# First constant on ScalarE's queue, transposes of w_out one item later, and a second copy buffer for the norm of w_in

## The chip, the cores and the metric

The kernel runs on one core of one Trainium2 chip. The metric is the device time of one execution in microseconds (us). Before the change it took 1651.17 us, the median of 3 runs (1646.57 to 1651.53). One execution was recorded by the hardware profiler; it took 1647.89 us, and its span, from the first instruction to the last, is 1646.1 us.

Engine names: PE is TensorE's matmul, PEld its weight load, ACT is ScalarE, DVE is VectorE, POOL is GpSimd, SP is SyncE, which here only issues DMAs (SPq in the trace). ACT issues DMAs too (ACTq).

## The reference, cut to what matters

```python
# batch 8, seq 3072, dim 256; float32 in and out
X  = rfft(x, axis=1)                        # along the sequence
Yr = shrink(Xr @ w_r - Xi @ w_i + b_r)      # shrink: sign(v) * max(|v| - 0.01, 0)
Yi = shrink(Xr @ w_i + Xi @ w_r + b_i)
a  = irfft(Yr + 1j * Yi, axis=1)            # 24576 tokens x 256
y  = (s * relu(a @ w_in) ** 2 + b) @ w_out  # w_in 256x2048, w_out 2048x256
e  = argmax(y @ w_gate)                     # 8 experts; at most 768 tokens of each are kept
out = gate * (relu(y @ w1[e]) @ w2[e])      # for the tokens kept, zero for the rest
```

The inputs w_in and w_out come as 64-bit floats, so the kernel turns their words into 32-bit floats itself, piece by piece.

## The kernel before, in words

All instructions are issued in the order in which the Python code emits them; every engine works through its own queue in that order, and waits stop the whole queue. A tile with a tag and a number of buffers waits until the oldest tile with that tag has been used up.

**The head (lines 1686 to 1701).** `f1_load(0, t)` loads the 16 slices of the first batch on SP's queue (192 KB each). `load_consts` then loads the constant `f1` (96x96 floats, 36 KB; `f<-c_f` in the trace) and `f1t`, and `load_moe` three small inputs, all on SP's queue. `f1_mm(0, t)` multiplies a slice by `f1` on PE (two passes of 512 columns), ACT or DVE in turn copies the result to a tile `z`, and SP writes it to DRAM (`zd<-z`). After slice 4 a 512 KB load of `d` stands on SP's queue, after slice 7 the two 256 KB loads of `wm`. Then come `warm(18)`, matmuls on zeros, and `group_items(0)`: 12 groups, each of which loads `zp` from what was written to `zd`, transforms, mixes with w_r and w_i, and transforms back. The first load of `zp` needs all 16 slices written.

**The conversion of the weights.** `conv_items(seq, ahead)` makes a list of items; item n issues the load of piece n+ahead, then `conv_low` of piece n+1 (two ACT passes over the raw words, which wait for the load), then for w_in `conv_use` of piece n, or for w_out `conv_tr` of piece n-1 (a DMA of the piece to `wd` on SP, 4 transposes on PE into `pwt`, a copy `wt` on ACT) and `conv_gate` of piece n-2 (16 matmuls with w_gate, a transpose on DVE), and last `conv_word` of piece n+1 (four DVE operations, L543 to L550, and two POOL operations, L551 and L552, which finish the piece `cf`). The 8 pieces of w_in (CONV_A) run beside the groups. The list for the 8 pieces of w_out (CONV_B) has 12 items: the first two are issued at the end of the groups, the other ten stand in slots 0, 0, 1, 2, 3, 3, 4, 5, 6, 6 of the next stage (MOE_CONV_AT), in front of all else in their slot. `load_bias` follows in slot 7.

**The first units of the next stage.** For batch 0 a loop runs over 64 slots; in slot k `s_unit` multiplies a tile of tokens by a part of w_in on PE (`ph`), squares the relu on ACT and DVE (`r`, `qb`), and then the slot's other work follows: conversion items, the norm of w_in, from slot 4 the loads of the next batch, from slot 6 its `f1_mm`.

**The norm of w_in** (`gram_items`) is 32 items spread over slots 0 to 9: 16 times `turn` (4 transposes on PE into `pwg`, a copy `wgt` on ACT, one buffer) and `add` (4 matmuls of `wgt` by itself into `gram`), in the order turn 0, add 0, turn 1, add 1 and so on. After the 8th and the 16th `add`, ACT squares `gram` into a tile `gsq` of its own and DVE sums it.

Of the kernel before, what the change touches and what calls it, by code (L numbers as in the profile page):

```python
# [10 lines left out]
F32 = mybir.dt.float32  # L11
F32R = mybir.dt.float32r
# [8 lines left out]
N1 = 96  # L21
# [3 lines left out]
NF = FF // 128  # L25
# [20 lines left out]
CONV_B = tuple(range(8))  # L46
# [102 lines left out]
class Kern:  # L149
# [11 lines left out]

    def load_consts(self, cp):
        nc, I = self.nc, self.I
        self.f1 = cp.tile([N1, 96], F32, tag="f1", name="f1")
        nc.sync.dma_start(out=self.f1, in_=I["c_f1"])
        self.f1t = self.mo.tile([96, N1], F32, tag="f1t", name="f1t")
        nc.sync.dma_start(out=self.f1t, in_=I["c_f1t"])
        self.d = cp.tile([128, G, 128], F32, tag="d", name="d")
        self.e = cp.tile([128, G, 128], F32, tag="e", name="e")
        self.wm = [cp.tile([128, 2, C], F32, tag=f"wm{k}", name=f"wm{k}") for k in range(4)]  # L170
        self.bias = [cp.tile([128, C], F32, tag=f"bias{k}", name=f"bias{k}") for k in range(2)]
        self.l20 = cp.tile([128, 2, 32], F32, tag="l20", name="l20")
        nc.vector.memset(self.l20, 0.0)
# [309 lines left out]
    def cbuf(self, what, k):  # L483

        if what == "r":
            if k not in CONV_A:
                pool, tag, n = self.wk, "x", 4
            else:
                pool, tag, n = (self.mo, "cr", 1) if CONV_A.index(k) % 3 == 2 else (self.mo, "u", 3)
            return pool.tile([128, 512, 2], I32, tag=tag, name="cr", bufs=n)  # L490
        dt = F32 if what in "fm" else I32
        if k in CONV_A:
            if what == "f":
                return self.stage()[:, :512]
            pool = self.mo
            tag, n = dict(t=("ah", 2), p=("asq", 2), m=("cm", 2))[what]
        else:
            pool = self.wk
            tag, n = dict(t=("z", 4), p=("sl", 2), m=("v", 3), f=("zp", 3))[what]
        return pool.tile([128, 512], dt, tag=tag, name="c" + what, bufs=n)  # L500

    def conv_load(self, k):
# [80 lines left out]
                                 start=(h == 0), stop=(h == 1), skip_group_check=True)  # L583
        nc.vector.transpose(out=self.wog[:, 2 * k:2 * k + 2], in_=pg[:, 0:64].rearrange("p (k f) -> p k f", k=2))

    def conv_items(self, seq, ahead):
        def at(f, n):
            if 0 <= n < len(seq):
                f(seq[n])

        def step(n):
            at(self.conv_load, n + ahead)
            at(self.conv_low, n + 1)
            for f, lag in ((self.conv_use, 0), (self.conv_tr, 1), (self.conv_gate, 2)):
                if 0 <= n - lag < len(seq) and (seq[n - lag] < 8) == (lag > 0):
                    f(seq[n - lag])
            at(self.conv_word, n + 1)
        return [lambda n=n: step(n) for n in range(-ahead, len(seq) + (2 if seq[-1] < 8 else 0))]

    def load_bias(self, pp):  # L600
# [18 lines left out]
    def gram_items(self):  # L619


        nc = self.nc

        def turn(k, f):
            ps = self.psum("pwg")
            for m in range(4):
                ff, c = divmod(m, 2)
                nc.tensor.transpose(ps[:, m * 128:(m + 1) * 128],
                                    (self.win, self.wl)[k].bitcast(F32)[:, c, (f + ff) * 128:(f + ff + 1) * 128], self.ident)
            t = self.wk.tile([128, 2, 2 * 128], F32R, tag="kw", name="wgt", bufs=1)  # L630
            nc.scalar.copy(out=t.rearrange("p a c -> p (a c)"), in_=ps)
            self.wgt = t

        def add(k, f):
            if f == 0:
                self.gram = self.lp.tile([128, 512], F32, tag="lg", name="gram")
            for ff in range(2):
                for c in range(2):
                    nc.tensor.matmul(self.gram[:, c * 256:(c + 1) * 256], self.wgt[:, ff, c * 128:(c + 1) * 128], self.wgt[:, ff],
                                     start=(f + ff == 0 and c == 0), stop=(f + ff == NF - 1), skip_group_check=True)  # L640
            if f == NF - 2:
                sq = self.wk.tile([128, 512], F32, tag="kw2", name="gsq", bufs=1)
                nc.scalar.activation(out=sq, in_=self.gram, func=AF.Square)
                nc.vector.tensor_reduce(out=self.nrm[:, k:k + 1], in_=sq, axis=AX.X, op=ALU.add)
        it = []
        for k in range(2):
            for f in range(0, NF, 2):
                it += [lambda k=k, f=f: turn(k, f), lambda k=k, f=f: add(k, f)]
        return it

    def bound_items(self, pp, diff=False):
# [1003 lines left out]
    def run(self):  # L1655
        tc, nc, B = self.tc, self.nc, self.B
# [4 lines left out]
        with ExitStack() as es, tc.manual_schedule():  # L1661
# [6 lines left out]
            cp = e2.enter_context(tc.tile_pool(name="cp", bufs=1))  # L1668
# [18 lines left out]
            self.wl = pp.tile([128, 2, FF], F32R, tag="wl", name="wl")  # L1687
            self.zero = zero = pp.tile([128, C], F32, tag="zero", name="zero")
            nc.vector.memset(zero, 0.0)
            for t in range(16):  # L1690
                self.f1_load(0, t)
            self.load_consts(cp)
            self.load_moe(pp)
            conv = self.conv_items(CONV_A, 3)
            f1 = self.f1_items(0)
# [14 lines left out]
            for k, f in enumerate(gr):  # L1710
                f()
                if k in extra:
                    extra[k]()
                if k in FFT_CONV_AT:
                    conv.pop(0)()
                if not conv:
                    conv = self.conv_items(CONV_B, 2)
            self.warm(WARM_GROUPS)
            self.i2_load(0, 0)
            self.i2_load(0, 1)  # L1720
# [28 lines left out]
            for b in range(B):  # L1749
# [60 lines left out]
                for k in range(64):  # L1810
                    i, u = divmod(k, 8)
# [3 lines left out]
                    if k in ZERO_AT:  # L1815
                        for zi in range(math.ceil(nz * nzi / nzn), math.ceil(nz * (nzi + 1) / nzn)):
                            nc.sync.dma_start(out=ov[zi].rearrange("p (a c) -> p a c", a=2),
                                              in_=zero.unsqueeze(1).to_broadcast([128, 2, C]))
# [60 lines left out]
```

## Time and profile before

| | before |
|---|---|
| median of the runs | 1651.17 us (1646.57 to 1651.53, 3 runs) |
| the profiled execution | 1647.89 us, span 1646.1 us |
| PE busy | 1471.8 us (89% of the span), 9469 matmuls |
| PE weight loads | 1217.3 us (74%) |
| DVE / ACT / POOL busy | 953.6 (58%) / 814.1 (49%) / 268.1 us (16%) |
| moved by DMA | 230.03 MB, mean 140 GB/s |
| mean granted clock of TensorE | 0.966 |

PE is the busiest engine, and in most of the span its share is near full. A share says nothing of what a stage waits for: that is read from the waits and from the order of time. A granted clock of 1.00 is 2.4 GHz, 0.50 is 1.2 GHz; a matmul takes about twice as long at the lower one, and counts as busy for that long.

### The profile page before, as it was taken

How to read it: one execution, taken by the hardware profiler on the slowest of the kernel's cores; microseconds unless marked ns; L12 is line 12 of the kernel's file. 1: busy time of each engine (PE TensorE's matmuls, PEld its weight loads, DVE VectorE, ACT ScalarE, POOL GpSimd, SP SyncE). 2: the span in 40 equal slices, each digit the busy share in tenths (PEclk: the TensorE clock that was granted, in tenths of full speed). 3: DMA queues.
4: the chain of work that ended last, by engine and by line, in shares of the span. 5: the costliest groups of instructions: out<-in, count | busy, mean ns of one | idle time of the engine just before them, and what ended most of it. 6: DMA issues, size and time to landing. Idle time of an engine off the chain costs nothing. (4 is left out here: it accounts for less than half of the span.)

```text
span 1646.1 us, 26007 instructions
## 1 busy us (share of the span) xinstructions
PE 1471.8 (89%) x9469; PEld 1217.3 (74%) x9469; DVE 953.6 (58%) x2057; ACT 814.1 (49%) x1252; POOL 268.1 (16%) x235
## 2 busy tenths in 40 slices
PE   6986789999998799999999999999999988988865
PEld 3875568777877568867876887788688768977753
DVE  1856357645555767755765676577557686633510
ACT  1425544563334564476457446744764575632311
POOL 0534100110000040021012001300220161231020
PEclk9997999999999899999999999999999999999978
DMA  7635454562443365465446435644655347610035
GB/s 208 236 107 169 131 153 153 158 185 100 148 135 123 87 152 152 122 171 150 147 135 166 143 122 159 175 128 131 166 146 153 91 110 229 183 50 17 14 105 180
DMA packets 273572, 230.03 MB, mean 140 GB/s; under 512 B 120045, under 2 KB 228335, under 8 KB 273424
## 3 DMA queue, kind: packets, MB, share of 16 engines
q1 hardware_dynamic: 255776, 200.17, 42.5%
q10 hardware_dynamic: 13824, 25.17, 4.1%
q0 software_dynamic: 3824, 2.82, 0.7%
q8 instruction: 80, 1.31, 0.4%
q14 instruction: 68, 0.56, 0.1%
HBM read 114.18 MB, written 114.09 MB: 139 GB/s over the span
## 5 line engine op out<-in xcount | busy, mean ns | idle before, releaser
L723 PE MATMUL ph<-ah,win 128*128 128x384 f32 (+1 forms) x2048 | 489.5, 367 | 8.4 <-ACT r L728 7.8
L728 ACT ACTIVATE r<-ph 128x768 bf16<-128x768 f32 (+1 forms) x512 | 395.6, 784 | 165.9 <-PE ph L723 123.2
L729 DVE TENSOR_TENSOR qb<-r 128x768 bf16<-128x768 bf16 (+1 forms) x512 | 298.9, 585 | 298.2 <-ACT r L728 270.5
L723 PEld LDWEIGHTS ph<-ah,win 128*128 128x128 f32 x2048 | 344.9, 192 | 79.9 <-issue 41.6
L335 PE MATMUL pmx<-wm,l 128*128 128x256 f32 x1196 | 296.5, 386 | 17.1 <-DVE kb L345 9.6
L398 POOL TENSOR_TENSOR asq<-ah 128x768 bf16<-128x768 f32 x64 | 95.9, 1498 | 1045.7 <-ACT ah L394 967.5
L335 PEld LDWEIGHTS pmx<-wm,l 128*128 128x128 f32 x1196 | 220.9, 191 | 54.1 <-DVE kb L345 16.0
L392 PEld LDWEIGHTS pi<-f1t,u 96*128 96x128 f32 x1024 | 129.6, 196 | 17.8 <-issue 8.9
L392 PE MATMUL pi<-f1t,u 96*128 96x96 f32 x1024 | 134.1, 281 | 6.7 <-DVE l L262 4.3
L226 PE MATMUL pz<-x,f 96*96 96x512 f32 x240 | 126.6, 612 | 14.6 <-DMA f<-c_f 14.6
L261 ACT COPY l<-pf 128x512 f32<-128x512 f32 x84 | 49.2, 586 | 142.7 <-PE pf L253 142.3
L373 ACT COPY v<-pi 128x512 f32<-128x512 f32 x96 | 56.3, 587 | 125.5 <-PE pi L371 125.5
L371 PE MATMUL pi<-t,e 128*128 128x256 f32 x384 | 99.7, 383 | 5.2 <-DVE t L330 5.2
L253 PEld LDWEIGHTS pf<-d,zp 128*128 128x128 f32 x672 | 88.9, 193 | 11.6 <-issue 3.8
L253 PE MATMUL pf<-d,zp 128*128 128x128 f32 x672 | 90.0, 277 | 6.9 <-DMA zp<-zd 6.9
L408 DVE STREAM_TRANSPOSE at<-pi 128x384 f32<-128x384 f32 x128 | 74.1, 579 | 34.6 <-ACT ah L394 24.8
L394 ACT CAST ah<-pi 128x384 fp32r<-128x384 f32 x128 | 61.1, 479 | 57.3 <-PE pi L392 57.3
L234 ACT COPY z<-pz 96x512 f32<-96x512 f32 x120 | 69.8, 581 | 37.7 <-PE pz L226 29.8
L371 PEld LDWEIGHTS pi<-t,e 128*128 128x128 f32 x384 | 72.7, 191 | 17.6 <-DVE t L330 7.0
L330 DVE TENSOR_TENSOR t<-t,cl 128x512 f32<-128x512 f32 x96 | 72.1, 752 | 3.3
L877 POOL DMA_INDIRECT list<-c,x x64 | 65.9, 1029 | 45.1 <-DVE c L873 29.0
L759 ACT COPY ls<-lg 128x384 f32<-128x384 f32 (+1 forms) x64 | 52.8, 825 | 25.7 <-PE lg L746 15.5
(395 smaller groups left out, 1814.5 us busy)
## 6 DMA issues: line engine op xcount, KB each, us to landing
zd<-z SPq DMA_DIRECT2D x128, 192.0 KB
zp<-zd SPq DMA_DIRECT2D x96, 256.0 KB
vd<-v ACTq DMA_DIRECT2D x96, 256.0 KB
u<-vd SPq DMA_DIRECT2D x64, 384.0 KB
ad<-at SPq DMA_DIRECT2D x256, 96.0 KB
out<-zero SPq DMA_DIRECT2D x96, 256.0 KB
x<-x SPq DMA_DIRECT2D x120, 192.0 KB
sd<-stage SPq DMA_DIRECT2D x32, 256.0 KB
```

Of the source, the lines that this page charges most:

```text
L226: nc.tensor.matmul(o, self.f1, xs.rearrange("p a c -> p (a c)"), start=True, stop=True)
L234: nc.scalar.copy(out=z.rearrange("p a c -> p (a c)"), in_=o)
L253: nc.tensor.matmul(pv[:, h, :, gi * 64:gi * 64 + 64], zp[:, gi, h * 128:(h + 1) * 128], self.d[:, 2 * p + gi, :].rearrange("p (t m) -> p t ...
L330: nc.vector.tensor_tensor(out=t, in0=t, in1=cl, op=ALU.subtract)
L335: self.nc.tensor.matmul(o, part(h), w[:, h], start=start and h == 0, stop=stop and h == 1, skip_group_check=True)
L371: nc.tensor.matmul(ps[:, gi * C:(gi + 1) * C], self.e[:, 2 * p + gi], t[:, gi * C:(gi + 1) * C], start=True, stop=True)
L392: nc.tensor.matmul(ps[:, :TC].rearrange("p (a n) -> p a n", n=4)[:, :, n], u[:, n, h::2], self.f1t, start=True, stop=True)
L398: nc.gpsimd.tensor_tensor(out=self.asq[b, i], in0=af, in1=af, op=ALU.mult)
L408: nc.vector.transpose(out=self.ar[:, :, :, h], in_=self.at.pop((b, i, h))[:, :TC].rearrange("p (g c) -> p g c", c=32))
L723: nc.tensor.matmul(ps[:, j, :n], self.win[:, k, f], ah[:, k, t0:], start=(k == 0), stop=(k == 1))
L728: nc.scalar.activation(out=r, in_=ps[:, :, :n], func=AF.Relu)
L729: nc.vector.tensor_tensor(out=q, in0=r, in1=r, op=ALU.mult)
```

## The change

The load of `f1` is issued from ACT's queue as the first of all loads, ahead of the 16 slices on SP's. The w_out list is `conv_items(CONV_B, 3, 2)`: the load is three pieces ahead and `conv_low` and `conv_word` two pieces ahead of item n, so the list has 13 items; the pieces' tiles `f` alternate between the tags `zp` and `t`. In the norm of w_in `wgt` alternates between two tags, the order is turn 0, turn 1, add 0, turn 2, add 1 and so on, and `gsq` takes a buffer of the tag `lh`, which `wt` uses too.

```diff
     def load_consts(self, cp):
-        self.f1 = cp.tile([N1, 96], F32, tag="f1", name="f1")
-        nc.sync.dma_start(out=self.f1, in_=I["c_f1"])
...
-            tag, n = dict(t=("z", 4), p=("sl", 2), m=("v", 3), f=("zp", 3))[what]
+            tag, n = dict(t=("z", 4), p=("sl", 2), m=("v", 3), f=(("zp", "t")[k % 2], 3))[what]
...
-    def conv_items(self, seq, ahead):
+    def conv_items(self, seq, ahead, early=1):
...
             at(self.conv_load, n + ahead)
-            at(self.conv_low, n + 1)
+            at(self.conv_low, n + early)
...
-            at(self.conv_word, n + 1)
+            at(self.conv_word, n + early)
...
-            t = self.wk.tile([128, 2, 2 * 128], F32R, tag="kw", name="wgt", bufs=1)
+            t = self.wk.tile([128, 2, 2 * 128], F32R, tag=("kw", "kw2")[f // 2 % 2], name="wgt", bufs=1)
             nc.scalar.copy(out=t.rearrange("p a c -> p (a c)"), in_=ps)
-            self.wgt = t
+            self.wgt[k, f] = t
...
-                sq = self.wk.tile([128, 512], F32, tag="kw2", name="gsq", bufs=1)
+                sq = self.wk.tile([128, 512], F32, tag="lh", name="gsq", bufs=2)
...
-        it = []
-        for k in range(2):
-            for f in range(0, NF, 2):
-                it += [lambda k=k, f=f: turn(k, f), lambda k=k, f=f: add(k, f)]
+        self.wgt = {}
+        tiles = [(k, f) for k in range(2) for f in range(0, NF, 2)]
+        it = [lambda: turn(*tiles[0])]
+        for n, t in enumerate(tiles):
+            it += [lambda u=u: turn(*u) for u in tiles[n + 1:n + 2]] + [lambda t=t: add(*t)]
...
+            self.f1 = cp.tile([N1, 96], F32, tag="f1", name="f1")
+            nc.scalar.dma_start(out=self.f1, in_=self.I["c_f1"])
             for t in range(16):
                 self.f1_load(0, t)
...
-                    conv = self.conv_items(CONV_B, 2)
+                    conv = self.conv_items(CONV_B, 3, 2)
```

## Rows read from the trace of the kernel before

**Rows 1.** Waits of PE and SP: waiting, waited for: total us, times, longest.
```profile
PE gram L639 <- ACT wgt L631: 16.0, 12, 8.0
PE pz L226 <- DMA f<-c_f: 14.6, 1, 14.6
PE pwt L569 <- POOL cf L552: 2.0, 1, 2.0
...
SPq L566 <- POOL cf L552: 26.6, 6, 8.3
```

**Rows 2.** Timeline, 0 to 46 us: start, us, engine, operation, idle before.
```profile
0.75 0.87 SPq L214 DMA_DIRECT2D x<-x  x2
...
9.85 0.31 SPq L165 DMA_DIRECT2D f<-c_f  x1
...
12.71 0.39 SPq L469 DMA_DIRECT2D wg<-moe_w_gate  x1
...
14.56 3.73 PE L226 MATMUL pz<-x,f 96*96 96x512 f32 x4 [14.56 <-DMA f<-c_f]
...
26.52 5.46 SPq L236 DMA_DIRECT2D zd<-z  x8
...
30.72 7.93 PE L420 MATMUL warm<-zero 128*128 128x256 f32 x36
...
35.63 0.84 SPq L242 DMA_DIRECT2D zp<-zd  x2
...
38.55 0.68 PE L280 MATMUL pf<-d,zp 128*128 128x128 f32 x4
...
45.55 0.68 PE L280 MATMUL pf<-d,zp 128*128 128x128 f32 x4 [0.63 <-DMA zp<-zd]
```

**Rows 3.** Windows of the head: stretch, engines' busy us, granted clock, DMA share, GB/s.
```profile
2.40:9.50 7.10, 0.00 (x0) 0.00 (x0) 0.00 (x0) 0.00 (x0) 0.00 (x0) 1.00 0.98 281
...
14.50:26.00 11.50, 11.44 (x21) 4.25 (x22) 2.98 (x5) 2.91 (x5) 0.00 (x0) 1.00 0.47 127
26.00:33.50 7.50, 7.50 (x25) 4.28 (x24) 2.52 (x4) 1.74 (x3) 0.00 (x0) 1.00 1.02 338
```

**Rows 4.** Timeline, 127 to 153 us.
```profile
127.11 1.02 SPq L519 DMA_DIRECT2D cr<-moe_w_out  x2
...
131.85 0.67 ACT L530 ACTIVATE cm<-cr 128x512 f32<-128x512 f32 x1 [4.87 <-DMA cr<-moe_w_out]
...
132.98 0.57 ACT L571 COPY wt<-pwt 128x512 f32<-128x512 f32 x1
...
134.10 1.23 PE L639 MATMUL gram<-wgt 128*128 128x256 f32 x4 [8.00 <-ACT wgt L631]
...
136.91 1.22 PE L639 MATMUL gram<-wgt 128*128 128x256 f32 x4 [0.73 <-ACT wgt L631]
...
152.12 0.85 PE L569 MATMUL pwt<-ident,cf 128*128 128x128 f32 x4 [2.04 <-POOL cf L552]
```

**Rows 5.** Windows: stretch, busy PE, PEld, DVE, ACT, POOL, then clock, DMA, GB/s.
```profile
134.10:145.60 11.50, 10.04 (x56) 8.72 (x56) 2.97 (x7) 4.39 (x8) 4.36 (x4) 0.50 0.51 182
...
152.40:159.30 6.90, 6.17 (x52) 4.94 (x54) 6.28 (x9) 2.99 (x6) 3.27 (x3) 0.51 0.21 78
...
179.80:183.20 3.40, 3.40 (x13) 2.31 (x11) 0.21 (x1) 0.96 (x2) 0.00 (x0) 0.50 0.08 14
...
137.90:163.80 25.90, 20.94 (x183) 17.61 (x181) 18.58 (x30) 15.12 (x27) 10.96 (x8) 0.72 0.37 125
163.80:189.70 25.90, 19.20 (x153) 14.25 (x152) 6.88 (x22) 11.21 (x20) 4.04 (x3) 0.93 0.31 93
189.70:1646.10 1456.40, 1323.59 (x8626) 1099.14 (x8624) 855.08 (x1896) 747.45 (x1137) 209.53 (x183) 0.97 0.47 136
```

**Rows 6.** One tile (ct): its DVE and POOL instructions, ns min/median/max.
```profile
L543 DVE TENSOR_SCALAR ct<-cr x16: 383/420/1327, 44.9 to 159.8; 128x512 int32<-128x512 int32 x16
L545 DVE SCALAR_TENSOR_TENSOR ct<-cr,ct x16: 692/693/1648, 45.3 to 160.8; 128x512 int32<-128x512 int32 x16
```

More of the change, by code (lines that the diff above doesn't have):

```diff
@@ L636, in add @@
                 self.gram = self.lp.tile([128, 512], F32, tag="lg", name="gram")
+            t = self.wgt.pop((k, f))
             for ff in range(2):
                 for c in range(2):
-                    nc.tensor.matmul(self.gram[:, c * 256:(c + 1) * 256], self.wgt[:, ff, c * 128:(c + 1) * 128], self.wgt[:, ff],
+                    nc.tensor.matmul(self.gram[:, c * 256:(c + 1) * 256], t[:, ff, c * 128:(c + 1) * 128], t[:, ff],
                                      start=(f + ff == 0 and c == 0), stop=(f + ff == NF - 1), skip_group_check=True)
             if f == NF - 2:
-                sq = self.wk.tile([128, 512], F32, tag="kw2", name="gsq", bufs=1)
+                sq = self.wk.tile([128, 512], F32, tag="lh", name="gsq", bufs=2)
                 nc.scalar.activation(out=sq, in_=self.gram, func=AF.Square)
                 nc.vector.tensor_reduce(out=self.nrm[:, k:k + 1], in_=sq, axis=AX.X, op=ALU.add)
-        it = []
-        for k in range(2):
-            for f in range(0, NF, 2):
-                it += [lambda k=k, f=f: turn(k, f), lambda k=k, f=f: add(k, f)]
+        self.wgt = {}
[3 more added lines that the diff above has]
+            it += [lambda u=u: turn(*u) for u in tiles[n + 1:n + 2]] + [lambda t=t: add(*t)]
         return it
```

## The prediction

> **What bounds the kernel now.** I read the waits of PE first, because PE is busy in most of the span; then the order of time around the longest ones; then windows, for the clock and the other engines' load in those stretches. The waits name all three places that the change touches: PE stands 14.6 us at the start until `f1` lands, 16.0 us in 12 waits for the copy `wgt`, one of them 8.0 us, and once 2.0 us for a converted piece of w_out; SP stands 26.6 us in 6 waits for converted pieces [rows 1]. All of it lies before 189.7 us. After that PE is busy 1323.6 of 1456.4 us, 91% [rows 5], and everything there is issued relative to what went before. So what the first 190 us save I carry to the end one for one.
>
> **The head.** `f1` is issued at 9.85 us, behind the 16 slices, and lands at 14.56, 4.7 us later [rows 2]. Issued first on ACT's queue, at about 0.75 as SP's first load, with nothing ahead of it, it should land between 2.4 us, when the transfers already run at full share [rows 3], and 0.75 + 4.7 = 5.5 us, the old delay. I take 3.2, near the lower end, because the old delay had a backlog in it. PE's work on the slices took 30.72 - 14.56 = 16.2 us [rows 2], so it would end at 19.4 instead of 30.72, 11.3 us earlier. The slices don't hold it up: 16 times 192 KB are 3.15 MB, at 281 GB/s [rows 3] 11.2 us, a slice each 0.7 us, while PE takes 1.0 us for one.
>
> The groups don't start when PE is done, though, but when the slices are written. SP issues the writes behind its loads, and these end at 12.71 + 0.39 us [rows 2], less 0.7 for the moved `f1`: 12.4. From there the transfers are late next: 3.15 MB of writes, 0.52 of `d` and 0.52 of `wm` stand on SP's queue before the first `zp`, 4.19 MB, and at 338 GB/s, the rate at full share [rows 3], that is 12.4 us. Before, this traffic trickled for 11.5 us at a share of 0.47 while PE set the pace [rows 3]. Begun at 14.0 (the slices are in, the first writes under way), with half a microsecond for the last to land, it lets the first `zp` be issued at 27.0 instead of 35.63: 8.6 us, not 11.3. If SP needs for each of these 19 DMAs the 0.68 us that eight writes took (5.46 us [rows 2]; PE paced those), the last is issued at 25.3 and `zp` at 28.3, a gain of 7.3; if the transfers start at once at 12.9, 9.7.
>
> The groups begin 2.9 us after `zp` is issued (35.63 to 38.55 [rows 2]), so at 29.9. The warm matmuls (7.93 us [rows 2]) would end at 19.4 + 7.9 = 27.3, where they now reach up to the first group. That leaves a new hole of 2.6 us on PE. After an idle time of 2.04 us [rows 4] the granted clock stood at 0.51 for the next 6.9 us [rows 5]; the same here costs half of that, 3.4 us, and gives back the 0.63 that PE waits for the third `zp` [rows 2]: 2.8. I count it in full: the head gives 8.6 - 2.8 = 5.8 us (bounds 3.9 and 9.7, with and without the fall).
>
> A rule of the Trainium skill speaks against this part ("DMA: Bandwidth & Descriptors", section "Issuing engines are not separate DMA queues"): DMAs issued from different engines run on the same DMA engines and interleave, so a second issuing engine saves issue time alone. By that rule the other queue would be worth the 0.3 us of the issue. I read the gain off the place in the order, not off the queue; no row here shows a small load on one queue against a backlog on the other, and that is the third rival.
>
> **The w_out pieces.** Load, `conv_low` and `conv_word` of piece k keep their place: one index more ahead in a list one item longer is the same item. What moves is `conv_tr` and `conv_gate`, one item later, the write to `wd` with them; the last gate goes from slot 6 to slot 7, ahead of `load_bias`, which then sums one transpose of 0.25 us later, beside PE's 16 gate matmuls: nothing. So the 8.00 us stall stays. It is not made by the transposes: `conv_low` of the third piece stands on ACT until its load lands (4.87 us to 131.85, issued at 127.11 behind writes on SP), and the first `wgt` copy stands behind it [rows 4]. Neither moves. Only the copy `wt` of 0.57 us, which stood between, goes behind [rows 4]: 0.5 us. The wait of 2.0 us for a piece goes, since its transposes now come an item after POOL is asked for it [rows 4]. SP's 26.6 us of waits for pieces shrink too [rows 1]; what stood behind them, loads for slots further on, had PE waiting for none, so that is worth nothing. The added tiles find free buffers: `zp` and `t` have three each and the groups are done with them.
>
> **The norm.** Beside the long wait there are 11 of 0.73 us (16.0 - 8.0 = 8.0 [rows 1, 4]). With the next `turn` between, whose four transposes keep PE some 0.6 us, and often a unit too, I leave 0.1 each: 7.0 us (bounds 5 and 8). `gsq` in an `lh` buffer can hold a `wt` copy until DVE has summed it, 0.7 us, off PE's path.
>
> **The clock in this stretch.** It is low from 134.1 to 145.6, 152.4 to 159.3 and 179.8 to 183.2 us, with PE busy 10.0, 6.2 and 3.4 [rows 5]. The second follows the 2.04 us wait that goes: half of 6.2 is 3.1. The third follows a loose run of copy waits: I count 1 of 1.7. In the first PE works with holes of 0.73 us; closed, the clock may rise earlier: 1.5 (0 to 3). Sum 5.6 (0 to 7.8).
>
> **What the stretch takes back.** From 137.9 to 163.8 DVE is busy 18.6 of 25.9 us and ACT 15.1 [rows 5]. PE with its waits gone and its clock up wants this part some 10 us shorter, below DVE's 18.6. PE can run two units ahead of DVE, but not more: I take back 4.5 us (0, if DVE's own blocked time shrinks too, to 11).
>
> 0.5 + 2.0 + 7.0 + 5.6 - 4.5 = 10.6 us, bounds 4 and 16. With the head 16.4 us. On the profiled execution, 1647.9 (span 1646.1 and 1.8 around it), that is 1631.5. It lies 3.3 us below the median, and two of the three runs are at 1651, so I forecast from the median: 1651.2 - 16.4 = 1634.8 us.
>
> **The rivals.**
> - *The word chain becomes the bound.* DVE's words slow down beside POOL: L545 takes 0.69 us at best and 1.65 at worst, L543 0.38 and 1.33 [rows 6]. The same POOL work in a shorter stretch meets more of them. The Trainium skill ("SBUF — State Buffer", section "SBUF: two separate sides") has VectorE and GpSimd take a shared port by an exclusive lock and the loser block for the whole instruction; the maxima here agree with a wait of about a microsecond. If the five words of slots 1 to 4 met POOL in both of these operations, DVE would need up to 5 x 1.9 = 9.5 us more. PE then keeps only a third of the stretch's gain: 1641.
> - *The waits change place.* ACT works in order; a copy of the next `turn` now stands ahead of relu and `wt`. If PE waits there instead, 1.0 us in each of 8 slots, and the hole in the head costs twice, 4 us are left: 1647. Against it: the waits for `wt` are now too small to be among the long ones.
> - *`f1` lands behind the slices all the same*, so the head gives nothing: 1641. For it only that the transfers are saturated from 2.4 us [rows 3]; against it that nothing is queued at 0.75.
> - *More than forecast.* The hole in the head costs no clock and DVE takes nothing back: 24 us, 1627.
> - *Slower.* The clock doesn't come back after the 8 us stall. PE is busy some 43 us from 134.1 to 189.7, 19.6 of them at the low level [rows 5]; all of it low would be 23.6 us more at twice the time, less the 11 us of waits gone: 12.6 longer, and with the head's 5.8 some 7 slower: 1658. It decides in the first 12 us after the stall. Against it: with more holes than now it rose at 145.6.
>
> **How the numbers follow.** Forecast 0.55 (1629 to 1641 by its own bounds), word chain 0.17, moved waits 0.08, `f1` late 0.09, more 0.07, slower 0.04. From these the range is 1625 to 1646. A change of 0.3%, 5 us, is about what a measurement here tells from none. Faster by more: the forecast, word chain, late `f1` and more, 0.88, less a little for their tails: 0.87. Within: moved waits and that tail, 0.08. Slower: 0.05.
>
> **What would show it.** Right: `pz` starts at 3 to 4 us; `zp` is issued at about 27; a hole of 2 to 3 us before the first `pf`, with a clock of 0.5 behind it; the 8 us wait of `gram` for `wgt` still there, and most of the 0.73 us waits gone; no wait of `pwt` for `cf`; the last `gram` at about 173 instead of 189. Wrong: a first `pz` after 6 us; a late `zp` with DMA share below 0.9 between 14 and 27; waits of PE for `wt`, `r` or `cf` in place of `wgt`; DVE busy above 0.9 from 130 to 155; or a gain up to 190 us that later stages don't keep.

## The result, and the profile after

The changed kernel takes 1637.72 us, the median of 7 runs (1634.62 to 1641.85); the kernel before, run beside it, 1651.53 (7 runs, 1646.57 to 1658.61). The ratio is 0.9911, with a 95% interval of 0.9886 to 0.9937: faster by 0.9%. The profiled execution of after, at 1641.85 us (span 1640.1), is the longest of its seven; that of before, at 1647.89, is shorter than five of the seven beside it. The two traces therefore differ by only 6.0 us.

Waits of after: engine, waiting, waited for: total us, times, longest.

```profile
PE gram L638 <- ACT wgt L629: 7.5, 2, 7.1
PE pz L224 <- DMA f<-c_f: 3.7, 1, 3.7
PE pf L278 <- issue: 3.5, 1, 3.5
...
PE pwg L626 <- DVE wog L582: 2.5, 1, 2.5
PE pwt L567 <- DVE wog L582: 2.0, 1, 2.0
...
PE pg L580 <- DVE wog L582: 1.4, 1, 1.4
...
SPq L564 <- POOL cf L550: 15.9, 5, 4.8
```

Against [rows 1] the wait for `f1` has gone from 14.6 to 3.7 us. Of the twelve waits for `wgt` only the long one is left, with 0.4 us beside it, and the wait for `cf` is gone. There are two newcomers: 3.5 us ahead of `pf`, put down to `issue` (the profile names nothing that PE waited for; `pf` reads `zp`, which was issued 2.8 us earlier), and 5.9 us in three waits for `wog`.

Timeline of after, the head (start, us, engine, operation, idle before):

```profile
0.75 0.42 ACTq L1691 DMA_DIRECT2D f<-c_f  x1
...
3.67 3.73 PE L224 MATMUL pz<-x,f 96*96 96x512 f32 x4 [3.67 <-DMA f<-c_f]
...
20.48 7.93 PE L418 MATMUL warm<-zero 128*128 128x256 f32 x36
...
20.74 4.92 SPq L234 DMA_DIRECT2D zd<-z  x8
...
29.10 0.84 SPq L240 DMA_DIRECT2D zp<-zd  x2
...
31.91 0.68 PE L278 MATMUL pf<-d,zp 128*128 128x128 f32 x4 [3.49 <-issue]
```

Beside [rows 2], PE's work on the slices starts 10.9 us earlier, but `zp` is issued only 6.5 and the first `pf` starts 6.6 us earlier. The warm matmuls end at 28.41, so PE stands idle for 3.5 us.

Windows of after (stretch, busy us of PE, PEld, DVE, ACT, POOL, then clock, DMA share, GB/s):

```profile
13.50:29.10 15.60, 14.91 (x53) 9.28 (x51) 3.43 (x5) 2.36 (x5) 0.00 (x0) 1.00 0.90 280
14.00:27.00 13.00, 13.00 (x47) 8.21 (x46) 3.24 (x5) 2.33 (x4) 0.00 (x0) 1.00 0.99 311
...
33.60:37.00 3.40, 3.40 (x15) 3.13 (x15) 0.65 (x3) 0.45 (x1) 0.00 (x0) 0.50 0.67 208
122.40:132.60 10.20, 5.90 (x27) 5.90 (x28) 4.38 (x8) 5.34 (x10) 4.97 (x4) 0.50 1.02 367
126.70:172.40 45.70, 37.53 (x341) 32.58 (x342) 28.47 (x53) 26.23 (x48) 17.48 (x13) 0.86 0.47 157
149.70:153.10 3.40, 3.40 (x28) 3.07 (x30) 3.19 (x5) 1.66 (x4) 1.29 (x2) 0.50 0.30 102
172.40:1640.10 1467.70, 1330.15 (x8629) 1106.09 (x8627) 856.27 (x1896) 749.11 (x1137) 209.15 (x183) 0.97 0.47 135
```

The same two stretches of before, from its first `gram` matmul to its last, and from there to the end:

```profile
134.10:189.00 54.90, 42.51 (x341) 34.24 (x342) 25.63 (x52) 26.34 (x47) 17.55 (x13) 0.80 0.39 126
189.00:1646.10 1457.10, 1324.29 (x8628) 1099.43 (x8626) 855.08 (x1896) 748.01 (x1137) 209.53 (x183) 0.97 0.47 136
```

The stretch of the norm shrank by 9.2 us (54.9 to 45.7), the rest grew by 10.6 (1457.1 to 1467.7). The 341 matmuls of the stretch kept PE busy 5.0 us less, at a mean granted clock of 0.86 for 0.80, and PE's idle time fell by 4.2 us (12.4 to 8.2). VectorE needed 2.8 us more for nearly the same work (53 instructions for 52).

Where the time went can be told closely, since both kernels issue 9469 matmuls: I set the start of the n-th of one trace against the n-th of the other. After leads by 6.0 us at the end of the groups (the 400th, 104 us), by 16.7 at the 1250th (260 us of before), by 15.5 at the 7250th (1276 us), and by 6.0 at the last. The last 9.5 us are the surprise; 5.4 of them are lost between 1335 and 1385 us. The table under the experiments shows that every kernel traced loses in this way against this one execution of before.

Timelines there, after and then before:

```profile
1336.01 0.64 PE L767 MATMUL plt<-ident,ls 128*96 128x128 f32 x4 [2.13 <-ACT ls L759]
1336.40 0.94 PE L723 MATMUL ph<-ah,win 128*128 128x384 f32 x4
1337.19 3.28 PE L390 MATMUL pi<-f1t,u 96*128 96x96 f32 x16
1340.17 6.81 PE L723 MATMUL ph<-ah,win 128*128 128x384 f32 x24
```

```profile
1351.60 0.64 PE L767 MATMUL plt<-ident,ls 128*96 128x128 f32 x4 [2.06 <-ACT ls L759]
1352.00 0.94 PE L723 MATMUL ph<-ah,win 128*128 128x384 f32 x4
1352.78 2.01 PE L392 MATMUL pi<-f1t,u 96*128 96x96 f32 x16
```

The hole ahead of `plt` is the same in both, 2.13 and 2.06 us. After it the 16 `pi` take 2.01 us in before and 3.28 in after. The window of the next 6.8 us shows the low level in after, filled by its 28 matmuls, and full clock in before, as the second line has it:

```profile
1337.50:1344.30 6.80, 6.80 (x28) 6.54 (x28) 4.51 (x7) 4.16 (x7) 6.49 (x7) 0.50 0.11 39
1351.60:1358.40 6.80, 6.34 (x41) 5.65 (x41) 5.56 (x9) 5.61 (x10) 6.41 (x7) 1.00 0.27 85
```

### The profile page after: what moved, and what is told of

It reads as the page before. It is cut to its first block, busy times and chain, and to the rows that moved or that the text cites. A ratio compares the mean times of both kernels' runs of the same rounds, so it can differ in the third digit from the quotient of the medians.

```text
span 1640.1 us, 26008 instructions
## 1 busy us (share of the span) xinstructions
PE 1474.6 (90%) x9469; PEld 1223.8 (75%) x9469; DVE 957.3 (58%) x2057; ACT 814.6 (50%) x1252; POOL 267.8 (16%) x235
## 5 line engine op out<-in xcount | busy, mean ns | idle before, releaser
L333 PE MATMUL pmx<-wm,l 128*128 128x256 f32 x1196 | 297.1, 387 | 17.4 <-DVE kb L343 9.6
```

The source lines that it names most:

```text
L333: self.nc.tensor.matmul(o, part(h), w[:, h], start=start and h == 0, stop=stop and h == 1, skip_group_check=True)
```

## The experiments

"Lead" is that of the n-th matmul over before's profiled execution, at the end of the groups and at the 1250th; the difference of the two is called the stretch's gain. Ratios are to the kernel before on the same chip. The leads of all thirteen traces in us, that at the last matmul too (added warm matmuls are left out of the count):

| trace | end of the groups | 1250th matmul | last matmul |
|---|---|---|---|
| the change: first, second, third | 6.0, 6.3, 6.6 | 16.7, 14.2, 12.5 | 6.0, 4.4, 3.9 |
| head alone | 6.2 | 3.8 | -2.4 |
| norm alone | 0.4 | 9.1 | 5.4 |
| w_out pieces alone | 0.0 | -5.0 | -13.0 |
| all but the w_out pieces | 8.5 | 16.7 | 9.2 |
| third load earlier | 6.4 | 17.4 | 8.9 |
| third load earlier, w_out part undone | 8.8 | 21.0 | 11.2 |
| 26 warm pairs | 8.5 | 13.9 | 8.5 |
| `wm` later | 7.2 | 14.1 | 3.8 |
| earlier load, w_out part undone, 23 warm pairs: twice | 7.8, 8.2 | 19.0, 19.8 | 12.3, 10.7 |

**The changed kernel unaltered, twice more**, to see what one execution is worth. No edit.

> The changed kernel once more, for a second profile and more times. Theory: the profiled execution lost some 9 us after 1340 us that belong to that execution, not to the change, so a second profile keeps the 15 to 16.5 us by which the matmuls ran ahead at 200 us up to about 1600 us, and the ratio stays near 0.991. Rival: the loss around 1340 to 1372 us comes from the change (transfers that now meet others); then it stands in this profile too, 5 us or more.

Measured: 0.9916 (0.9891 to 0.9941), leads 6.3 and 14.2.

> The changed kernel unaltered, beside the next run on the same chip. Theory (its gain in the stretch of the first units differs from execution to execution with where the clock falls, 10.7 and 8.0 us so far): a gain of 5 to 11 us between the end of the groups and 200 us, 6 to 9 us at the end of the groups, ratio to before 0.989 to 0.994.

Measured: 0.9934 (0.9912 to 0.9955), leads 6.6 and 12.5. So three executions of the same instructions have stretches' gains of 10.7, 8.0 and 5.9 us. Two more kernels have the same instructions there, those with 26 warm pairs and with `wm` later: 5.4 and 6.9. Windows of the second and the third execution, from the first `gram` matmul to the last, and of the longest low clock within the third's:

```profile
127.00:174.40 47.40, 39.13 (x341) 33.56 (x342) 29.14 (x53) 26.31 (x48) 17.59 (x13) 0.81 0.47 151
127.40:174.80 47.40, 39.09 (x341) 33.49 (x342) 29.12 (x53) 26.35 (x48) 17.59 (x13) 0.81 0.47 151
145.70:155.90 10.20, 7.94 (x51) 7.14 (x50) 8.42 (x11) 3.32 (x6) 6.62 (x6) 0.50 0.38 124
```

PE's idle time in the stretch is 8.3 us in both, 8.2 in the first trace and 12.4 in before: the waits give 4.1 to 4.2 us in every execution. PE's busy time is where they differ: it fell by 5.0 us in the first trace, at a mean clock of 0.86, and by 3.4 in the two others, at 0.81. The rest of the difference lies outside these windows. Between 1335 and 1385 us the three lost 5.4, 4.4 and 3.3.

**The head alone.** Only the load of `f1` as changed; conversion and norm as before.

```diff
-        nc.sync.dma_start(out=self.f1, in_=I["c_f1"])
...
+            nc.scalar.dma_start(out=self.f1, in_=self.I["c_f1"])
```

> Only the load of f1 moved to ScalarE's queue, all else as before. Theory: the first matmul at 3.7 us, the first zp issued at 29.1, a hole of 3.5 us before the groups with the clock low once after it, the groups' end and everything up to 110 us 6.0 us earlier, time 6 us less (1645 against 1651). Rival: a start moved this early is lost again at the stall of the gram copies at 126 us, which waits for a load; then less than 3 us.

Measured: 0.9956 (0.994 to 0.9973), about 7.3 us of 1656; lead 6.2 at the end of the groups, of which its trace keeps 3.8 to the 1250th matmul; the waits for `wgt` (16.5 us) and `cf` (3.2) are no shorter than before. The hole is longer here:

```profile
31.90 0.93 PE L278 MATMUL pf<-d,zp 128*128 128x128 f32 x4 [4.11 <-issue]
```

**The norm alone.** `wgt` with two tags, the turns one ahead and `gsq` in a buffer of `lh`; the rest as before.

```diff
+            t = self.wk.tile([128, 2, 2 * 128], F32R, tag=("kw", "kw2")[f // 2 % 2], name="wgt", bufs=1)
...
+            it += [lambda u=u: turn(*u) for u in tiles[n + 1:n + 2]] + [lambda t=t: add(*t)]
```

> Only the norm of w_in changed (two copy buffers, turn n+1 ahead of add n, gsq in an lh buffer); head and w_out pieces as before. Theory: the 11 waits of 0.73 us go, the clock comes back sooner, 7 to 9 us less (1642 to 1644); the wait of pwt for a piece, 2.0 us, stays. Rival: the gram waits turn into waits for the pieces or for the transposes of wog, and less than 4 us are left.

Measured: 0.9933 (0.9908 to 0.9958), about 11.1 us (7 to 15). Its waits:

```profile
PE gram L640 <- ACT wgt L631: 6.3, 2, 6.0
PE pwt L569 <- POOL cf L552: 4.7, 2, 3.0
```

The eleven short waits are gone without any help from the other parts; the wait for `cf`, which the change was to remove, grew from 2.0 to 4.7.

**The w_out pieces alone**, with `early` and the two tags of `f` as in the change.

```diff
-                    conv = self.conv_items(CONV_B, 2)
+                    conv = self.conv_items(CONV_B, 3, 2)
```

> Only the w_out pieces changed (transposes one item later, pieces alternate between two tags). Theory: the wait of pwt for a piece goes, and with it the low clock behind it, 2 to 4 us less. Rival: PE waits instead for the transpose of wog on VectorE, as in the changed kernel (5.9 us in 3 waits), and the part gives nothing or costs up to 2 us.

Measured: 1.0018 (0.9996 to 1.004): nothing, or a little worse. The wait for `cf` is gone, and `gram` waits at least as long as in [rows 1] (the view ends at 190 us; a twelfth wait of 0.7 us follows):

```profile
PE gram L639 <- ACT wgt L631: 16.9, 11, 8.7
```

There is no wait for `wog` here; PE waits 2.3 us for `at` and 0.9 for `wt` at `pg` instead. The three parts alone come to -7.3, -11.1 and +3.0, together -15.4 us; the whole came to -14 beside the same runs of before. The intervals of the parts, 3 to 4 us to either side, leave room for the difference.

**All but the w_out pieces.** The call above, undone in the changed kernel; the two tags of `f` stay.

> The changed kernel with the w_out pieces put back (conv_items(CONV_B, 2), so one piece ahead; f1 on ScalarE's queue and the two copy buffers stay). Theory: the pieces' part is worth nothing here: the w_out part alone gave a ratio of 1.002, so without it the time is the changed kernel's or 1 to 3 us less, 14 to 18 us under before (ratio 0.989 to 0.9915); PE waits for a piece (pwt for cf, 2 to 5 us) in place of the 5.9 us for wog. Rival: with the gram waits gone the transposes need the lead, and the kernel loses 4 us or more of the gain (ratio 0.994).

Measured: 0.9911 (0.9892 to 0.993), as the whole change. Its waits:

```profile
PE gram L638 <- ACT wgt L629: 7.9, 2, 7.6
PE pwt L567 <- POOL cf L550: 4.7, 2, 4.2
```

Without this part PE waits 4.7 us for `cf`, with it 5.9 for `wog`. In the whole change it moved a wait and did not remove one. How, the timeline of after shows:

```profile
139.89 1.36 POOL L550 TENSOR_TENSOR cf<-cf,ct 128x512 f32<-128x512 f32 x1
140.13 1.67 DVE L543 SCALAR_TENSOR_TENSOR ct<-cr,ct 128x512 int32<-128x512 int32 x1
...
143.04 0.24 DVE L582 STREAM_TRANSPOSE wog<-pg 128x64 f32<-128x64 f32 x1
...
143.43 0.63 PE L567 MATMUL pwt<-ident,cf 128*128 128x128 f32 x4 [1.97 <-DVE wog L582]
```

`pwt`, `pwg` and `pg` take turns in the same PSUM buffers. The one that `pwt` wants is freed by the transpose of `wog` on VectorE, and that stands behind the words of a piece, one of which takes 1.67 us beside POOL for 0.69 at best.

**The third piece's load an item earlier**, in the changed kernel. The rows of after show where the 7.1 us stall comes from, as in [rows 4]:

```profile
120.57 1.02 SPq L517 DMA_DIRECT2D cr<-moe_w_out  x2
...
124.94 0.68 ACT L528 ACTIVATE cm<-cr 128x512 f32<-128x512 f32 x1 [4.52 <-DMA cr<-moe_w_out]
...
126.08 1.05 ACT L629 CAST wgt<-pwg 128x512 fp32r<-128x512 f32 x2
...
126.70 1.22 PE L638 MATMUL gram<-wgt 128*128 128x256 f32 x4 [7.15 <-ACT wgt L629]
```

```diff
-            at(self.conv_load, n + ahead)
+            if n == first:
+                at(self.conv_load, n + ahead)
+            at(self.conv_load, n + ahead + (n >= first and first > -ahead))
...
-                    conv = self.conv_items(CONV_B, 3, 2)
+                    conv = self.conv_items(CONV_B, 3, 2, -2)
```

> The changed kernel, but the load of the third w_out piece is issued together with that of the second, ahead of the writes ad<-at. Theory: the stall of gram at 119.6 to 126.7 us is that load alone, so ScalarE goes on at once, the wait of 7.1 us shrinks to 2.5 us or less, the clock stays up or comes back sooner, and the last gram ends 5 to 9 us earlier than in the changed kernel: 5 to 9 us under it (ratio to before 0.985 to 0.988). Rival: the words on VectorE and POOL take over, and less than 3 us are gained.

Measured: 0.992 (0.9893 to 0.9947), leads 6.4 and 17.4. The stall shrank as it should, and the waits for `wog` stayed what they were, 5.8 us for 5.9. The last `gram` starts at 170.1 us, against 172.2, 174.2 and 174.6 in the three executions of the change: 2 to 4.5 us earlier, where 5 to 9 were expected, and the ratio doesn't tell the two kernels apart. Its waits:

```profile
PE pwg L628 <- DVE wog L582: 5.8, 2, 3.3
PE gram L640 <- ACT wgt L631: 2.0, 2, 1.7
```

**The same with the w_out part undone.** `conv_items(CONV_B, 2, 1, -1)`.

> The changed kernel with its w_out part undone (transposes one item behind the conversion, as before) and the load of the third w_out piece issued one item earlier. Theory (VectorE's word chain sets the pace of slots 0 to 4, so whatever one wait loses another takes over): the 7.1 us stall of gram for wgt falls to under 2.5, but PE waits 4 us or more for cf or wog in place of it; first 200 us at most 1.5 us shorter than in the changed kernel; ratio to before 0.990 to 0.993. Rival (the waits are independent of each other): the stall falls by 5 and the others stay, so the stretch is about 5 us shorter, last gram at about 167 instead of 172, ratio about 0.988.

Measured: 0.9886 (0.9868 to 0.9905), leads 8.8 and 21.0, last `gram` at 167. Its waits:

```profile
PE pwt L567 <- POOL cf L550: 7.0, 4, 3.7
...
PE gram L640 <- ACT wgt L631: 2.1, 2, 1.8
```

Waits for `cf` of 7.0 us took the place of those for `wog`, as the theory said, but the ratio and the last `gram` came where the rival put them. This trace alone does not decide it: 2.8 of the 5 us by which the last `gram` is earlier than in the first trace of the change were there at the end of the groups, ahead of the edit. The stretch's gain, 12.2, is 1.5 us above the first trace's, and 4.2 and 6.2 above the two others'.

**More warm matmuls.** `WARM_F1 = 26` for 18 in the changed kernel.

> The changed kernel with 26 warm matmuls after the slices in place of 18, 3.5 us more at full clock, so that the hole of 3.5 us ahead of the first group is filled with work. Theory: the groups start at the same time, 31.9 us, but the clock stays at 1.00 there, and the groups' end comes 0.6 to 1.7 us earlier. Rival: the groups at their start wait for transfers anyway (third zp), and nothing moves; or the warm matmuls run past the landing of zp and cost what they overrun.

Measured: 0.9929 (0.9915 to 0.9942), no better. The lead at the end of the groups is 8.5, but two kernels with the old 18 pairs have 8.5 and 8.8 too. The first group starts later than in after, right behind the last warm matmul, and the clock stays up:

```profile
21.16 11.39 PE L418 MATMUL warm<-zero 128*128 128x256 f32 x52
...
32.38 0.61 PE L278 MATMUL pf<-d,zp 128*128 128x128 f32 x4
```

**`wm` loaded behind the first two `zp`.**

```diff
-            pre = {4: lambda: self.load_d(0), 7: self.load_mix}
+            pre = {4: lambda: self.load_d(0)}
...
             gr.pop(0)()
+            self.load_mix()
```

> The changed kernel with the two loads of wm (0.52 MB) issued behind the first two loads of zp in place of ahead of the last eight writes. Theory: between 13.5 and 29.1 us the transfers are the bound, so 0.52 MB less ahead of zp lets it be issued 1.5 us earlier, at 27.5, and the first pf at 30.3; the mixing then waits for wm, so of this at most 1 us is kept. Rival: SP's issue of the writes sets it; then zp moves by the two issues, 2 us and more, or not at all if the copies of the slices set it.

Measured: 0.9912 (0.9896 to 0.9928). `zp` went out 2.1 us earlier, and a later `zp` took most of that back. The 2.1 decide nothing between theory and rival: 0.52 MB at the 280 GB/s of after are 1.9 us, and the two issues of `wm` take 1.9 us in after. Timeline:

```profile
26.97 0.83 SPq L240 DMA_DIRECT2D zp<-zd  x2
...
30.20 0.68 PE L278 MATMUL pf<-d,zp 128*128 128x128 f32 x4 [2.24 <-DMA zp<-zd]
...
38.60 0.68 PE L278 MATMUL pf<-d,zp 128*128 128x128 f32 x4 [2.03 <-DMA zp<-zd]
```

**The version with the earlier load, without the w_out part, and five more warm pairs**, on two chips; the second time beside the changed kernel.

```diff
-WARM_F1 = 18
+WARM_F1 = 23
...
-                    conv = self.conv_items(CONV_B, 3, 2)
+                    conv = self.conv_items(CONV_B, 2, 1, -1)
```

> The kernel of the run before this one with five more of the warm-up matmul pairs (WARM_F1 23 for 18), to cover the hole ahead of the first group without running past the first zp. Theory (the hole costs only its low clock, about 0.6 to 1.5 us): no clock at 0.5 between 29 and 36 us, groups' end 0.5 to 1.5 us earlier than without, ratio lower by 0.001 or less, which can't be told. Rival (the hole still costs what was predicted, 2.8 us, and more behind it): ratio lower by 0.002 or more.

Measured: 0.9866 (0.9845 to 0.9887). It is 0.002 under the run without the warm pairs, but the intervals overlap; the clock stays up ahead of the first groups, and the lead at their end, 7.8, is no larger.

> The changed kernel with the w_out part undone, the load of its third piece an item earlier and WARM_F1 23, again, now on the same chip as the changed kernel. Theory (the early load takes 5 us off the stall and the waits for pieces give 2 back, the longer warm-up is worth 1): 0.985 to 0.989 of before, and 0.3 to 0.6% (5 to 9 us) under the changed kernel. Rival (the difference seen so far is one of chips and executions): within 0.2% of the changed kernel.

Measured: 0.989 (0.9874 to 0.9906), median 1636.73 us; the unaltered change on that chip 1643.53. So it is 6.8 us or 0.41% faster than the change (ratio of the means 0.9957, interval 0.9936 to 0.9977) and beats both kernels. Which of its three edits carries how much of that isn't separated. But in the table the four traces with the earlier load have the largest gains in the stretch, 11.0 to 12.2 us; the six with the head's and the norm's parts and the late load have 5.4 to 10.7. Its longest waits in the stretch:

```profile
PE pwt L567 <- POOL cf L550: 5.3, 3, 3.7
...
PE gram L640 <- ACT wgt L631: 1.7, 2, 1.4
PE pf L278 <- issue: 1.4, 1, 1.4
```

## Why the prediction was right, and where it was not

The forecast was 1634.8 us with a range of 1625 to 1646; 1637.72 lies 2.9 above the one and inside the other.

- **`f1` lands early.** `pz` starts at 3.67 us (forecast 3.2, bounds 2.4 and 5.5), so the rival of the late `f1` is out. Behind the slices the same load landed at 14.56 [rows 2]. Whether `f1` first on SP's queue would do as well wasn't tried. By the rule of the Trainium skill ("DMA: Bandwidth & Descriptors", section "Issuing engines are not separate DMA queues") a second issuing engine saves only the time of the issue. The 10.9 us measured at `pz` come with an earlier place too, so they neither confirm nor contradict it.
- **When `zp` goes out.** 29.10 us instead of 27.0. Two steps failed. The rate: I let 4.19 MB go at 338 GB/s, and from 14 to 27 us it was 311 at a share of 0.99, which is 1.1 us. And the half microsecond for the last write to land: from 27.0, where the transfers thin out, to the issue of `zp` it was 2.1 us. The prediction's second way, by SP's issues, came nearer: 28.3, with the last issue done at 25.3 (25.66 measured). Which of the two set the time isn't separated; that PE no longer did was right: it was done with the slices at 20.5, 8.6 us before `zp`.
- **The hole.** 3.5 us for 2.6, as `zp` was later. Its clock cost was put at 2.8; in the first trace the clock was low for only 3.4 us behind it, and the lead went from 6.6 at the start of the groups to 6.0 at their end. So 8.6 - 2.8 became 6.6 - 0.6: a sum of 5.8 against 6.0, from two terms each 2 us off, which cancel by luck. Seven traces with this same head have 6.0 to 8.8 there; the ratio of the part alone gives 7.3.
- **The norm.** Seven us for the eleven waits: all but 0.4 us of them went. The part alone gave 11.1 (7 to 15), more than any other.
- **The w_out pieces.** Here the prediction was wrong by its own steps. It gave 0.5 + 2.0 us, and the clock behind that wait, 3.1, to this part; alone it measured +3.0 (-0.7 to +6.6), and left out of the whole it cost nothing. The wait for `cf` went, as said. What the prediction had nothing for is that the transposes then wait for their PSUM buffer behind VectorE's words, other than in the general amount of 4.5. That wait for `wog` stands only in the traces that have this part together with the norm's; neither alone shows it.
- **The clock in the stretch.** 5.6 us (0 to 7.8) was a sum over three falls. The first, behind the stall, held 11.5 us of the stretch in before and 5.9, 4.6 and 4.7 in the three executions; that was forecast, with 1.5 us. The second should have gone with the wait for `cf`: it held 6.9 us in before, and the second low time of the three executions 3.4, 10.2 and 10.2, so this step failed. The third stayed at 3.4. In all PE's busy time in the stretch fell by 5.0, 3.4 and 3.4 us. With the mean clock at 0.81 for 0.80 in the last two, not all of their 3.4 can be the clock's; what the rest is stays open. A term that hangs on where the clock falls should have been put lower, with both ends kept.
- **Taken back.** 4.5 us forecast; the three waits for `wog` are 5.9. With the 2.0 and the 7.0 the forecast for PE's idle time in the stretch was 4.5 us less; 4.1 to 4.2 were measured in all three executions. The rival of the word chain is partly true: PE now waits for VectorE, which needed 2.8 us more and was busy 22.0 of the 25 us from 130 to 155, 0.88, just under the 0.9 that the prediction named as a sign against it. Over the whole stretch it was not the bound, busy 28.5 of 45.7 us: with the load earlier, three kernels without the w_out part gained 11.2 to 12.2 us there, where the one with the late load gained 8.2.
- **The stall of 8 us** stayed, at 7.1 (6.3 and 6.7 in the two other traces), for the reason given: the load of the third piece. With it loaded an item earlier the stall fell to 1.7.
- **Sum.** 16.4 us forecast; the lead was 16.7 at 260 us in the first trace, 14.2 and 12.5 in the next two. That the first comes within 0.3 us of the forecast is luck. By the ratios the three sets of runs gave 14.7, 13.9 and 10.9 us.
- **"Carried to the end one for one"** held to 1338 us in the first trace (15.5 of 16.7). There the clock fell behind a hole that didn't lower it in before. But all thirteen traces lose, between 260 us and the end, 3.7 to 10.7 us against this one execution of before. It took 1647.89 us, 3.6 to 9.2 less than the medians of before beside the runs here, so a good part of the loss is likely its own; that is not shown, as there is no second trace of before. By the medians the changed kernel was faster by 13.8, 13.5 and 11.2 us, against leads of 16.7, 14.2 and 12.5 at 260 us. Between 1335 and 1385 us the three executions of the changed kernel lost 3.3 to 5.4 us, the w_out part alone 3.0, the kernels with the norm alone and with 26 warm pairs (which hold the norm's part and the whole change) 0.2 and 0.6. So the change does not force the fall there; that it is more frequent with it isn't excluded, and this stays open.

## What to carry to other kernels

A small load that everything waits for belongs ahead of the bulk, and its worth is read at the next thing that becomes late, here the writes and not the matmuls. A wait that is taken away by issuing one step later can come back at the buffer that the step needs, as here, so ask which engine's queue releases it and what stands ahead in it. The same instructions gained 5.4 to 10.7 us in one stretch: compare several traces before a term is believed, and of the kernel before too, since a lead against one execution carries that execution's luck.

## What the runs showed of the hardware that was not expected

Holes of the same length on PE, 2.06 us in before and 2.13 in after, at the same instruction, were followed by full clock in one and by 6.8 us at 0.50 in the other. The same 341 matmuls of the stretch kept PE busy 37.5, 39.1 and 39.1 us in three executions of one kernel, at a mean granted clock of 0.86, 0.81 and 0.81. One VectorE word took 1.67 us beside a POOL operation of 1.36 and 0.69 at best, as in [rows 6].
